# Seven products of quarters for eight in three of the six blocks of the last batch's wide product

## The chip, the cores and the metric

One core of one Trainium2 chip runs the whole kernel. The metric is the device time of one execution in microseconds (us), as the median over several runs. The profile is of one execution, with times in us from the start of its span. A core has five engines with a line of instructions each: TensorE (PE) multiplies, with its weight loads (PEld) beside it; VectorE (DVE), ScalarE (ACT) and GpSimd (POOL) work on elements; SyncE (SP) issues transfers, as ScalarE and GpSimd also do. Each engine takes its instructions in order. Between engines there are semaphores. Matmul results go to eight banks of 128 x 512 fp32; all else is in the large on-chip buffer, SBUF.

## The reference

A recurrent attention with decay (4 batches, 8 heads, 768 tokens, 64 channels a head) feeds a mixer over tokens and then one over channels:

```python
state = gamma[None, :, None, None] * state + np.einsum('bhd,bhe->bhde', k[:, :, t], v[:, :, t])
y[:, :, t] = scale * np.einsum('bhd,bhde->bhe', q[:, :, t], state)
...
xt = x.transpose(0, 2, 1)                       # x: 4 x 768 x 512
h = np.maximum(xt @ w_tok1, 0.0) @ w_tok2       # 768 -> 256 -> 768
u = x + h.transpose(0, 2, 1)
h2 = np.maximum(u @ w_ch1, 0.0) @ w_ch2         # 512 -> 1536 -> 512
return (u + h2).astype(np.float32)
```

The change is in `u @ w_ch1`, called the wide product here, for the last of the four batches. `h2`'s second half, from 1536 back to 512, is called the narrow product.

## The kernel before

**Planned order.** The kernel doesn't emit its work as it is written. It first makes a list of `Op`s, each with a priority, the engines it may run on with an estimated cost for each, the ops it depends on, the buffers it takes (`Slot`, with a tag) and uses. `arrange()` plans an order from the list greedily: at the earliest time at which something can start, it takes the op of best priority on that engine, picks an engine where there are several, a bank where one is needed, and a buffer of the tag when the oldest is given back. `guard` adds time to an op's earliest start, `behind` holds it back until another op is planned. `replay()` then runs through the order with a model of the transfers and gives a time. This is done 16 times with the transfers' times fed back, then once for each number in `SEEDS`, where `shake()` sets random delays on a few of the ops. The order with the best modelled time is emitted. So each engine's whole line, from the first instruction on, comes from this plan.

**Stages.** `front(b, p)` does the attention and the token mixer of batch b for the head pair p (four pairs of 128 channels). It leaves `X` (u in fp32, tokens on partitions) and `UT` (u in fp16, transposed: channels on partitions, four blocks `p` of 768 tokens). For batches 2 and 3 the transposing is done by a transfer that SyncE issues (line 752). L735 adds the token mixer's result to X; L656 and L743 are fp16 casts, mostly on GpSimd.

`back(b)` does the channel mixer. `widen(sh)` makes, for a half `sh` of the tokens (384 of 768), twelve blocks `ft` of 128 hidden channels: four matmuls of 128x384 over the four channel blocks into one bank (L818), then a relu on ScalarE to fp16 (L832) into `H2[:, ft]`. A batch has 24 such blocks, 96 matmuls. The tag `h2` has two buffers, one for each half of the tokens, and both are in use until the batch before has done its narrow product.

Batches 0 and 1 use `narrow(sh)` (L860, with its sum at L869). Batches 2 and 3 (`SEVEN = 2`) use `narrow_seven()`. There the matrices are cut into quarters (two halves of tokens, two halves of hidden channels, two halves of outputs), and Winograd's form of Strassen's method gives the four output quarters by seven products for eight, with some sums ahead and behind:

- `differences()`, L790: sums T1 to T4 of the quarters of `w_ch2`, on VectorE, 12 instructions, once, with the lowest priority
- `s_op`, L896: sums S1 to S4 of the quarters of H2, on VectorE, for two hidden blocks (and their two partners six blocks on) at a time: 12 instructions for each batch, in the tiles `kf`, `qf`, `v` and in H2 itself
- L937: seven products of six matmuls of 128x256 for each tile `i` of 128 tokens: p1 first (it needs only the lower halves), then others with the sums; S2 (tile `qf`), S1 (`kf`) and S4 (`v`) are their operands
- L964, L947, L990: a copy of p1's bank on ScalarE, and the sums of the products with X and with each other on VectorE, with GpSimd as an alternative for some; L955 stores

The banks have tags with ranges: `back` for banks 3 to 7, `seven` for all eight.

**Priority.** `front` ops have priority (0, ...), those of `back` (1, b, number in the batch), `differences` (2, ...).

Of the kernel before, what the change touches and what calls it, by code (L numbers as in the profile page):

```python
# [11 lines left out]
FP = mybir.dt.float32  # L12
F16 = mybir.dt.float16
AF = mybir.ActivationFunctionType
ALU = mybir.AluOpType
# [3 lines left out]
def kernel(  # L19
# [11 lines left out]
    nc = tc.nc  # L31
    B, H, S, D = q.shape
    P = 128
    NC = S // P
    HC = NC // 2
    NP = H // 2
    C = H * D
# [3 lines left out]
    NF = DC // P  # L41
    SH = S // 2
# [10 lines left out]
                uT=3, h2=2, o=4, w1=2)  # L53
    BANKS = dict(first=range(0, 7), front=range(0, 5), back=range(3, 8), seven=range(0, 8), fill=range(7, 8))
    SEM = 80
    XB, XU = 2, 2
    UNT, UW = 1, P
    QR, QH, TN = (0,), (1,), 3
    SEEDS = [20002, 20003, 20007, 20226]
    SPLIT, T1_AT, T2_AT = 1, 3, 4  # L60
    XS, M4 = 1, 3
    EARLY, BOTH_FIRST, SEVEN = 0, 1, 2
# [206 lines left out]
    def tile_of(slot, shape, dtype):  # L269
        if slot.bank is not None:  # L270
            slot.tile = ps.tile(shape, dtype, name=f"bank{slot.bank}", bufs=1)
        else:
            slot.tile = sb.tile(shape, dtype, name=slot.tag, bufs=BUFS[slot.tag])
        return slot.tile

    def act(n):
        t = 178 + 81 * n // 100
        return t - 100, t
# [7 lines left out]
    def one(eng, cost, emit):  # L286
        return [(eng, cost[0], cost[1], emit)]

    def either(emit, **costs):
        return [(e, c[0], c[1], lambda emit=emit, e=e: emit(e)) for e, c in costs.items()]  # L290
# [22 lines left out]
    def emit():  # L313
        nc.gpsimd.iota(away, pattern=[[1, P]], base=0, channel_multiplier=-1,
                       allow_small_or_imprecise_dtypes=True)
# [35 lines left out]
    NW = 3  # L351
    FW = NF // NW
    wc1 = [const_p.tile([P, NP, FW * P], F16, name=f"wc1_{i}") for i in range(NW)]
    wc2 = [const_p.tile([P, FW, C], F16, name=f"wc2_{i}") for i in range(NW)]
    wops = {}
# [15 lines left out]
    loads, x_done, uT_done, y_done, t2_done = {}, {}, {}, {}, {}  # L371
# [53 lines left out]
    def front(b, p):  # L425
# [154 lines left out]
        for blocks in runs:  # L580
            A = [Slot(FA) for _ in blocks]

# [215 lines left out]
    def back(b):  # L798
        X, UT = Xs[b], UTs[b]
        seq = [0]  # L800

        def op(ways, deps=(), takes=(), uses=(), dma=None):
            seq[0] += 1
            return Op((1, b, seq[0]), ways, deps, takes, uses, dma=dma)
        h2_of = {}

        def widen(sh):
            H2 = Slot("h2")
            rel = []
            fts = [f + g for f in range(0, NF // 2, 2) for g in (0, 1, NF // 2, NF // 2 + 1)]  # L810
            for ft in (fts if b >= SEVEN else range(NF)):
                A = Slot("back")

                def emit(cts, sh=sh, ft=ft, A=A):
                    acc = tile_of(A, [P, 512], FP) if cts[0] == 0 else A.tile
                    w = wc1[ft // FW]
                    for ct in cts:
                        nc.tensor.matmul(acc[:, :SH], w[:, ct, (ft % FW) * P:(ft % FW + 1) * P],  # L818
                                         UT.tile[:, ct, sh * SH:(sh + 1) * SH],
                                         start=(ct == 0), stop=(ct == NP - 1))  # L820
                cts = list(range(NP))
                c1 = None
                for part in (cts[:NP // 2], cts[NP // 2:]):
                    c1 = op(one("PE", (326, 480), lambda e=emit, q=part: e(q)),
                            [uT_done[b, p, sh] for p in (part if SPLIT > b else range(NP))] + [wops["c1", ft // FW], c1],
                            [A] if c1 is None else [], [UT] if c1 is None else [UT, A])

                def emit(e, ft=ft, A=A, H2=H2):
                    if H2.tile is None:
                        tile_of(H2, [P, NF, SH], F16)  # L830
                    if e == "ACT":
                        nc.scalar.activation(H2.tile[:, ft], A.tile[:, :SH], AF.Relu)  # L832
                    else:
                        nc.vector.tensor_scalar(H2.tile[:, ft], A.tile[:, :SH], 0.0, None, ALU.max)
                rel.append(op(either(emit, ACT=act(SH)),
                              [c1] + rel[:1], [H2] if ft == 0 else [], [A] if ft == 0 else [A, H2]))
            h2_of[sh] = H2, rel

        def narrow(sh):
            H2, rel = h2_of[sh]  # L840
# [168 lines left out]

        fts_of = [f + g for f in range(0, NF // 2, 2) for g in (0, 1, NF // 2, NF // 2 + 1)]  # L1010
        if b >= SEVEN:
            widen(0)
            widen(1)
            narrow_seven()
        elif b < BOTH_FIRST:
            widen(0)
            widen(1)
            narrow(0)
            narrow(1)
        else:  # L1020
            for sh in range(2):
                widen(sh)
                narrow(sh)
# [27 lines left out]
    for b in range(B):  # L1051
        back(b)
# [9 lines left out]
    best = None  # L1062
    for turn in range(16 + len(SEEDS)):
        if turn >= 16:
            shake(SEEDS[turn - 16])
        try:
            order = arrange()
            t = replay(order)
# [51 lines left out]
```

## Time and profile before

| What | Value |
|---|---|
| Median of 7 runs | 199.29 us (197.61 to 199.98) |
| The profiled execution | 199.98 us, of which the span is 198.2 us |
| Mean granted TensorE clock | 0.997 |
| Instructions | 4910 |
| Busy, TensorE / weight loads | 188.0 us (95%), 1951 matmuls / 130.9 us |
| Busy, VectorE | 131.2 us (66%) |
| Busy, ScalarE | 112.6 us (57%) |
| Busy, GpSimd | 82.7 us (42%) |
| Last transpose of the last batch's u (L752) | issued at 146.0 us, 2.7 us from issue to landing |
| Wide product of batch 3 (L818) | 12 matmuls from 154.2 us, 84 from 166.5 to 180.2 us |
| Narrow product of batch 3 (L937) | 180.2 to 194.1 us |

A matmul's busy time (326 ns for 128x384) is longer than the time from one to the next (84 of them take 13.65 us), since they overlap; a VectorE, ScalarE or GpSimd instruction also overlaps a little with the next. Therefore a price from a row is the time from start to end of one, and a price in a full line is the distance from one to the next. A wait is read from the idle time ahead of an instruction and its releaser.

### The profile page before, as it was taken

How to read it: one execution, taken by the hardware profiler on the slowest of the kernel's cores; microseconds unless marked ns; L12 is line 12 of the kernel's file. 1: busy time of each engine (PE TensorE's matmuls, PEld its weight loads, DVE VectorE, ACT ScalarE, POOL GpSimd, SP SyncE). 2: the span in 40 equal slices, each digit the busy share in tenths (PEclk: the TensorE clock that was granted, in tenths of full speed). 3: DMA queues.
4: the chain of work that ended last, by engine and by line, in shares of the span. 5: the costliest groups of instructions: out<-in, count | busy, mean ns of one | idle time of the engine just before them, and what ended most of it. 6: DMA issues, size and time to landing. Idle time of an engine off the chain costs nothing.

```text
span 198.2 us, 4910 instructions
## 1 busy us (share of the span) xinstructions
PE 188.0 (95%) x1951; PEld 130.9 (66%) x1951; DVE 131.2 (66%) x338; ACT 112.6 (57%) x251; POOL 82.7 (42%) x118
## 2 busy tenths in 40 slices
PE   7778899999999999899999999999999999999991
PEld 3456697566686675477575664576767787657881
DVE  6599681017899997757685925567289687048972
ACT  4368667899857664578642675248765002875000
POOL 7996876389789953427452210212320010000001
PEclk9999999999999999999999999999999999999998
DMA  7999999999999999999999991732030024100223
GB/s 120 144 169 177 209 205 207 177 155 149 149 149 179 170 160 198 130 201 168 135 157 88 221 158 36 171 71 40 20 65 3 0 106 159 56 0 0 106 110 106
DMA packets 97654, 24.89 MB, mean 126 GB/s; under 512 B 90208, under 2 KB 94688, under 8 KB 97632
## 3 DMA queue, kind: packets, MB, share of 16 engines
q0 software_dynamic: 73136, 13.18, 95.4%
q1 hardware_dynamic: 20896, 5.38, 21.3%
q10 hardware_dynamic: 3600, 6.03, 9.0%
q8 instruction: 15, 0.25, 0.6%
q14 instruction: 7, 0.06, 0.1%
HBM read 26.74 MB, written 6.29 MB: 167 GB/s over the span
## 4 chain that ended last, share of the span: by engine, by line
PE 57%; DMA 25%; POOL 8%; DVE 4%; issue 3%; ACT 0%; DVEq 0%; POOLq 0%
PE bank L818 24%; PE bank L937 14%; DMA kf<-in_k_dram 12%; DMA wc<-in_moe_w_ch_dram 9%; PE bank L860 9%; DMA wt<-in_moe_w_tok_dram 4%; POOL v L388 3%; PE bank L728 3%; PE bank L670 3%; PE bank L591 2%; PE bank L625 1%; POOL qf L406 1%; PE bank L621 1%; POOL kf L388 1%; POOL x L656 1%
## 5 line engine op out<-in xcount | busy, mean ns | idle before, releaser
L818 PE MATMUL bank<-uT,wc 128*128 128x384 f16 x384 | 69.3, 326 | 0.0
L832 ACT ACTIVATE h<-bank 128x384 f16<-128x384 f32 x96 | 45.3, 492 | 22.1 <-PE bank L818 16.0
L818 PEld LDWEIGHTS <-wc 128*128 128x128 f16 x384 | 35.6, 98 | 20.6
L860 PE MATMUL bank<-wc,h 128*128 128x512 f16 x144 | 36.7, 379 | 0.0
L605 DVE TENSOR_TENSOR am<-bank,mask 128x384 f16<-128x384 f32 x64 | 32.4, 549 | 4.8 <-PE bank L591 4.6
L656 POOL CAST x<-X 128x384 f16<-128x384 f32 x25 | 12.7, 511 | 30.3 <-ACT X L639 26.5
L639 ACT ACTIVATE X<-bank,gy 128x192 f32<-128x192 f32 x58 | 20.6, 419 | 6.0 <-PE bank L625 5.9
L735 DVE TENSOR_TENSOR X<-X,bank 128x384 f32<-128x384 f32 x30 | 15.8, 549 | 9.9 <-PE bank L728 9.7
L553 DVE SCALAR_TENSOR_TENSOR U<-U,gp,bank 128x128 f32<-128x128 f32 (+1 forms) x64 | 20.9, 326 | 1.5
L743 POOL CAST u<-X 128x384 f16<-128x384 f32 x27 | 13.4, 516 | 17.7 <-DVE X L735 17.5
L860 PEld LDWEIGHTS <-h 128*128 128x128 f16 x144 | 12.3, 98 | 9.5
L388 POOL DMA_DIRECT2D v<-in_v_dram x16 | 16.5, 1029 | 4.4 <-DMA kf<-in_k_dram 1.9
L564 ACT ACTIVATE r<-U 64x320 f16<-64x320 f32 x31 | 14.5, 467 | 5.9 <-DVE U L553 5.5
L388 POOL DMA_DIRECT2D kf<-in_k_dram x15 | 15.3, 1020 | 5.2 <-DMA qf<-in_q_dram 3.6
L937 PEld LDWEIGHTS <-h 128*128 128x128 f16 x144 | 14.1, 98 | 1.8
L670 PE MATMUL bank<-x,wt 128*128 128x128 f16 x192 | 13.6, 219 | 1.1 <-POOL x L656 0.8
L990 POOL TENSOR_TENSOR o<-o,w 128x256 f32<-128x256 f32 x1 | 1.0, 963 | 32.2 <-DVE w L947 32.2
L670 PEld LDWEIGHTS <-wt 128*128 128x128 f16 x192 | 11.9, 98 | 3.4 <-issue 1.6
L625 PEld LDWEIGHTS <-am 128*128 128x128 f16 x192 | 12.3, 98 | 2.9 <-DVE am L605 0.2
L625 PE MATMUL bank<-v,am 128*128 128x64 f16 x192 | 14.0, 193 | 0.0
L466 ACT ACTIVATE k<-kf,gk 128x384 f16<-128x384 f16 x16 | 9.8, 613 | 6.4 <-DMA kf<-in_k_dram 4.7
L728 PE MATMUL bank<-h,wt 128*128 128x128 f16 x180 | 13.3, 219 | 0.0
(93 smaller groups left out, 273.0 us busy)
## 6 DMA issues: line engine op xcount, KB each, us to landing
out_dram<-o ACTq DMA_DIRECT2D x22, 256.0 KB, 3.2
v<-in_v_dram POOLq DMA_DIRECT2D x16, 192.0 KB, 9.6
wc<-in_moe_w_ch_dram POOLq DMA_DIRECT2D x6, 512.0 KB, 15.4
kf<-in_k_dram POOLq DMA_DIRECT2D x15, 192.0 KB, 9.4
qf<-in_q_dram POOLq DMA_DIRECT2D x12, 192.0 KB, 8.9
wt<-in_moe_w_tok_dram POOLq DMA_DIRECT2D x2, 384.0 KB, 9.7
qf<-in_q_dram POOLq DMA_DIRECT2D x8, 96.0 KB, 8.7
X<-in_k_dram SPq DMA_DIRECT2D x1, 384.0 KB, 3.6
```

What stands on the lines that cost most here:

```text
L388: nc.gpsimd.dma_start(out=tile_of(s, [P, 2, NC, D], F16), in_=src[b, 2 * p:2 * p + 2].rearrange("h (c p) d -> p (h c) d", p=P))
L553: nc.vector.scalar_tensor_tensor(U[:, c, :W], U[:, c - 1, :W], gp[:, p:p + 1], o, ALU.mult, ALU.add)
L605: nc.vector.tensor_tensor(am[:, :m], src, k_, ALU.mult)
L625: nc.tensor.matmul(o[:, j * D:(j + 1) * D], M.tile[:, m], V.tile[:, j, c], start=(c == 0), stop=(c == 0 or j == 1))
L639: nc.scalar.mul(X.tile[:, half(hf), h * D:(h + 1) * D], yv[:, :, j * D:(j + 1) * D], gy[:, h:h + 1])
L670: nc.tensor.matmul(acc[:, jt * P:(jt + 1) * P], wt1[:, i, jt * P:(jt + 1) * P], X16.tile[:, i], start=(i == 0), stop=(i == NC - 1))
L728: nc.tensor.matmul(acc[:, i * P:(i + 1) * P], wt2[:, jt, t], H1.tile[:, jt], start=(jt == 0), stop=(jt == NJ - 1))
L735: nc.vector.tensor_tensor(xo, xo, T2.tile[:, :HC * P].rearrange("p (i d) -> p i d", d=P), ALU.add)
L818: nc.tensor.matmul(acc[:, :SH], w[:, ct, (ft % FW) * P:(ft % FW + 1) * P], UT.tile[:, ct, sh * SH:(sh + 1) * SH], start=(ct == 0), stop=(c ...
L832: nc.scalar.activation(H2.tile[:, ft], A.tile[:, :SH], AF.Relu)
L860: nc.tensor.matmul(A.tile, H2.tile[:, ft, i * P:(i + 1) * P], wc2[ft // FW][:, ft % FW], start=(opens and ft == 0), stop=(ft == NF - 1), s ...
L937: nc.tensor.matmul(bank.tile[:, cols], lhs(f, t), rhs(f), start=(f == 0 and not adds), stop=(f == HF - 1), skip_group_check=adds)
```

## The change

For batch 3 (`WIDE = 3`), `widen(0)` and `widen(1)` are replaced by `widen_seven()`. The six pairs of hidden blocks (q, q + 6) are each one small matrix product of quarters: two halves of tokens (`tok`), two halves of the channels that are summed over (`HP` = 2 blocks of 128 each), and the two hidden blocks q and q + 6. For q in `QUADS` = 1, 2, 4 the four output blocks (q and q + 6, both halves of tokens) come from seven products of two matmuls each; for q = 0, 3, 5 they are made as before, by `unit`, though in banks of the tag `seven`.

For the seven products there are sums ahead: T1 to T4 of the quarters of UT (four VectorE instructions of 128x768 fp16, in a buffer of tag `uT`), and S1 to S4 of the quarters of `w_ch1`'s blocks (three VectorE instructions of 128x256 fp16 each, in a buffer of tag `X`). T1 has a guard of 3000 ns in the plan. The sums of the weights have the priority (1, 2, 1) and are planned behind the first sum of batch 3's token mixer.

`quad` then has for each q the seven products in four banks, one copy on ScalarE, five VectorE sums in fp32 (two partial, three that are outputs), and four relus: one on ScalarE from a bank, three from SBUF on ScalarE or GpSimd (`relus`). `out` uses buffers of the tags k16, q16, kT and qT, which the attention no longer needs.

The relus of the other batches are as before; `unit` and `put` are `widen`'s body in functions of their own. `SEEDS` has four other numbers, so the plan of the whole kernel is drawn anew.

```diff
+    WIDE, QUADS, T_LATE = 3, [1, 2, 4], 3000
...
-    SEEDS = [20002, 20003, 20007, 20226]
+    SEEDS = [50147, 50148, 50150, 50217]
...
+            def bb(r, c):
+                return UT.tile[:, r * HP:(r + 1) * HP, tok[c]]
+
+            def aa(q, r, c):
+                ft = q + r * HF
+                return wc1[ft // FW][:, c * HP:(c + 1) * HP, (ft % FW) * P:(ft % FW + 1) * P]
+
+            def mix(k, todo, deps, m=1):
+                slot = T if k[0] == "T" else W
+                first = [made[x] for x in made if x[0] == k[0]][:1]
+
+                def emit():
+                    if slot.tile is None:
+                        tile_of(slot, [P, NP, S] if slot is T else [P, NC, 2 * C], F16)
+                    for o, x, y, alu in todo():
+                        nc.vector.tensor_tensor(o, x, y, alu)
+                made[k] = op(one("DVE", (200 * m, 200 * m + 90) if m > 1 else (480, 560), emit),
+                             deps + first, [] if first else [slot], ([slot] if first else []) + ([UT] if slot is T else []))
+                if k == "T1":
+                    made[k].guard = T_LATE
+                if slot is W:
+                    made[k].prio = (1, 2, 1)
+                    made[k].behind = x_done[B - 1, 0, 0]
...
+            mix("T1", lambda: [(tv("T1"), bb(0, 1), bb(0, 0), ALU.subtract)], ud)
+            mix("T2", lambda: [(tv("T2"), bb(1, 1), tv("T1"), ALU.subtract)], ud + [made["T1"]])
+            mix("T3", lambda: [(tv("T3"), bb(1, 1), bb(0, 1), ALU.subtract)], ud)
+            mix("T4", lambda: [(tv("T4"), bb(1, 0), tv("T2"), ALU.subtract)], ud + [made["T2"]])
...
+            mix("S1", each(lambda i, q: (wv("S1")[:, :, i], aa(q, 1, 0), aa(q, 1, 1), ALU.add)), cd, n)
+            mix("S2", each(lambda i, q: (wv("S2")[:, :, i], wv("S1")[:, :, i], aa(q, 0, 0), ALU.subtract)),
+                cd + [made["S1"]], n)
+            mix("S3", each(lambda i, q: (wv("S3")[:, :, i], aa(q, 0, 0), aa(q, 1, 0), ALU.subtract)), cd, n)
+            mix("S4", each(lambda i, q: (wv("S4")[:, :, i], aa(q, 0, 1), wv("S2")[:, :, i], ALU.subtract)),
+                cd + [made["S2"]], n)
+
+            def quad(i, q):
+                A, Bk, Ck, Dk = (Slot("seven") for _ in range(4))
+                W1, U2, U3 = Slot("u16"), Slot("x16"), Slot("x16")
...
+                p1 = mm(A, lambda c: aa(q, 0, 0)[:, c], lambda c: bb(0, 0)[:, c], True, ud + cd, [UT])
+
+                def emit():
+                    nc.scalar.copy(tile_of(W1, [P, SH], FP), A.tile[:, :SH])
+                w1 = op(one("ACT", act(SH), emit), [p1], [W1], [A])
+                p6 = mm(Bk, sv("S2"), lambda c: tv("T2")[:, c], True, [made["S2"], made["T2"]], [W, T])
+                u2 = add(U2, W1, Bk, [w1, p6], [])
+                p5 = mm(Ck, sv("S1"), lambda c: tv("T1")[:, c], True, [made["S1"], made["T1"]], [W, T])
+                p2 = mm(A, lambda c: aa(q, 0, 1)[:, c], lambda c: bb(1, 0)[:, c], False, [w1], [UT])
+                put(q, H2[0], rel[0], [p2], [A], lambda: A.tile[:, :SH], dict(ACT=act(SH)))
+                p4 = mm(Dk, lambda c: aa(q, 1, 1)[:, c], lambda c: tv("T4")[:, c], True, cd + [made["T4"]], [T])
+                p7 = mm(Bk, sv("S3"), lambda c: tv("T3")[:, c], False, [u2, made["S3"], made["T3"]], [W, T])
+                u3 = add(U3, W1, Bk, [p7], [])
+                relus = dict(ACT=act(SH), POOL=(500, 580))
+
+                def out(sh, ft, x, bank, deps):
+                    o = Slot(("k16", "q16", "kT", "qT")[temps[0] % 4])
+                    temps[0] += 1
+                    d = add(o, x, bank, deps, [])
+                    put(ft, H2[sh], rel[sh], [d], [o], lambda: o.tile, relus)
+                    return d
+                c22 = out(1, q + HF, U3, Ck, [u3, p5])
+                p3 = mm(Ck, sv("S4"), lambda c: bb(1, 1)[:, c], False, [c22, made["S4"]], [W, UT])
+                out(0, q + HF, U3, Dk, [u3, p4])
+                out(1, q, U2, Ck, [u2, p3])
+            for q in range(HF):
+                if q in QUADS:
+                    quad(QUADS.index(q), q)
+                else:
+                    for ft in (q, q + HF):
+                        for sh in range(2):
+                            unit(sh, ft, H2[sh], rel[sh], "seven")
...
         if b >= SEVEN:
-            widen(0)
-            widen(1)
+            if b >= WIDE:
+                widen_seven()
+            else:
+                widen(0)
+                widen(1)
             narrow_seven()
```

## The prediction

> **What bounds the kernel now.** I read the chain of waits first, from its end, because it says which engine the end hangs on. Its last pieces are (start, length, what):
>
> ```profile
> 144.46 6.50 PE bank L818 x40
> 150.96 3.27 PE bank L937 x30
> 154.24 1.95 PE bank L818 x12
> 156.19 10.48 PE bank L937 x96
> 166.67 13.65 PE bank L818 x84
> 180.32 13.78 PE bank L937 x132
> 194.12 0.29 DVE o L947
> 194.41 0.20 DVEq L1115
> ```
>
> From 144 us to 194 us one TensorE matmul follows another; no piece is a wait. L818 is the wide product, L937 the narrow one by sevens. The last batch's wide product is the 12 matmuls at 154.24, put in while the batch before waited for its sums, and the 84 at 166.67: 96 in all, and 13.65 / 84 = 0.1625 us each. So the change works on a stage where each matmul less moves the end by 0.1625 us, if no wait takes its place.
>
> Then the stretches, to see what the other engines have left (columns: busy time and count of each engine, clock, DMA share, GB/s):
>
> ```profile
> core 0: us, PE busy (x) PEld busy (x) DVE busy (x) ACT busy (x) POOL busy (x), PEclk, DMA share, GB/s
> 0.00:85.00 85.00, 78.88 (x929) 53.64 (x929) 59.34 (x176) 57.64 (x122) 62.41 (x83) 1.00 2.02 167
> 129.50:145.10 15.60, 15.60 (x186) 11.21 (x184) 8.48 (x19) 10.78 (x27) 4.19 (x9) 1.00 0.20 48
> 145.10:155.40 10.30, 10.30 (x76) 7.17 (x74) 10.24 (x25) 5.64 (x12) 0.90 (x2) 1.00 0.11 21
> 155.40:166.50 11.10, 11.10 (x101) 9.75 (x100) 8.62 (x19) 1.24 (x3) 0.73 (x1) 1.00 0.25 94
> 166.50:180.15 13.65, 13.65 (x86) 8.22 (x84) 4.59 (x11) 9.71 (x21) 0.00 (x0) 1.00 0.11 40
> 180.15:194.20 14.05, 13.94 (x134) 12.40 (x131) 11.61 (x26) 1.65 (x5) 0.90 (x1) 1.00 0.20 76
> ```
>
> TensorE is full in every row behind the first, at full clock. VectorE has no time left from 145.1 to 155.4 (0.06 us idle), and its large hole is in the stage that is changed: 13.65 - 4.59 = 9.06 us. GpSimd does nearly nothing behind 147 us.
>
> Last the groups and the forms, for the prices (minimum/median/maximum of one, in ns, for the lines with slashes):
>
> ```profile
> L832 ACT ACTIVATE h<-bank 128x384 f16<-128x384 f32 x96 | 45.3, 492 | 22.1 <-PE bank L818 16.0
> L735 DVE TENSOR_TENSOR X<-X,bank 128x384 f32<-128x384 f32 x30 | 15.8, 549 | 9.9 <-PE bank L728 9.7
> L656 POOL CAST x<-X 128x384 f16<-128x384 f32 x25 | 12.7, 511 | 30.3 <-ACT X L639 26.5
> L896 DVE TENSOR_TENSOR kf<-h x6: 543/550/557, 146.9 to 180.9; 128x768 f16<-128x768 f16 x6
> L790 DVE TENSOR_TENSOR wT<-wc x3: 410/464/718, 145.2 to 153.8; 128x512 f16<-128x512 f16 x3
> 181.47 0.56 DVE L896 TENSOR_TENSOR qf<-kf,h 128x768 f16<-128x768 f16 x1
> 182.77 0.82 PE L937 MATMUL bank<-wT,qf 128*128 128x256 f16 x6
> ```
>
> **The change, part by part.** *Matmuls.* Each of the three quads replaces four output blocks of four matmuls (16) by seven products of two (14), with the same 128x384 shape. 3 x 2 x 0.1625 = 0.975 us less on the path. The other 12 blocks keep their 48 matmuls; the stage goes from 96 to 90. This is the whole gain that the change can have in that stage, 0.49% of the median.
>
> *VectorE, sums of the quads.* Five for each quad (u2, u3 and three outputs), SBUF and bank in, 128x384 in fp32: the form of L735. One takes 0.549 us, and two in a row took 1.02 us, so a second costs 0.47. 15 sums are 7.05 us in a full row and 8.25 us if each must wait for the one ahead.
>
> *VectorE, sums of the tokens' halves (T1 to T4).* Four of 128x768 f16, the size of L896 at 0.55: 1.9 to 2.2 us.
>
> *VectorE, sums of the weights (S1 to S4).* Twelve of 128x256 f16, a size that the trace does not show. Above, L790 with 512 elements at 0.41 bounds it; below, the step from 512 to 768 elements (0.55 - 0.41 = 0.14 for 256) taken as if an instruction cost nothing but its elements. 12 x 0.14 = 1.7 us, 12 x 0.41 = 4.9 us; I take the straight line through the two rows, 0.27 each, 3.3 us. They depend on weights loaded long before, and on a buffer of tag X that batch 1 gives back when its last result sum ends, at 129.4. If they stand between 129.5 and 145.1 they lie in 15.60 - 8.48 = 7.1 us of hole and cost nothing. Queued behind them there are the front sums of the last batch; up to 3.3 us of delay to its tokens (the last transpose is issued at 146.0 and lands 2.7 us later) ends before their first use at 154.24. Without that hole they come behind 145.1 and are rival B.
>
> *ScalarE and GpSimd.* A copy of a 128x384 bank to fp32 for each quad is not shown; a 128x256 copy at 0.37 bounds it below, and I take L832's 0.49, which has its size, as the upper end. Of the 24 relus 15 stay with ScalarE and 9 may go to either. If all stay, 27 operations at 0.434 (seven in a row took 3.04) are 11.7 us in a stage of 12.7 to 14.6 us: hidden. On GpSimd a relu is costed at L656's 0.51, as cast of the same size; the one fp32 sum of 256 elements there took 0.73, which is the upper end. Both lie in an empty engine.
>
> The relus on GpSimd do meet VectorE: the first sum L790 at 145.2 ran beside a GpSimd cast and took 0.718 us against the usual 0.410, so a meeting costs 0.31 us. The quads' sums read one bank and one SBUF tile, as L735 does; at risk are the L896 sums, which read two SBUF tiles. Three meetings would be 0.9 us on VectorE's line; I take none into the sum, since ScalarE has room, and keep 0.9 for the upper end.
>
> The Trainium skill speaks against this part: "SBUF — State Buffer", section "Who interferes with whom", says that a VectorE instruction with two SBUF inputs and a GpSimd instruction that reads SBUF exclude each other for a whole instruction. By that rule each meeting costs up to a whole GpSimd relu, 0.51 us by the row above, where the one seen cost 0.31; the sum with three meetings would be 1.5 us in place of 0.9.
>
> *Chain inside a quad.* p1, copy, u2, p7, u3, c22, p3, an output sum, a relu: 0.49 + 0.49 + 0.55 + 0.49 + 0.55 + 0.55 + 0.49 + 0.55 + 0.49 = 4.65 us with rows' times (a pair of matmuls ends 0.326 + 0.1625 after its start), while its products fill TensorE for 14 x 0.1625 = 2.28 us. So two quads or a quad and plain blocks must run side by side. A quad takes four banks of eight, so that fits, and 12 plain blocks (7.8 us) are there to fill.
>
> *Hand-over to the narrow product.* Its third product needs the L896 sums of the last four blocks. Now qf is ready at 181.47 + 0.56 = 182.03 and used at 182.77: 0.74 us to spare. With VectorE behind by more than that, more of the first products of other tiles must be put in its place. For the waits that are left I choose 0.3 us: from 0 (the planner hides all) to 0.9 (the meetings above).
>
> *Queues and DMA.* No transfer is added or removed. H2's two buffers are held by batch 2's narrow product until 165.45, as now, so relus of blocks computed early wait, and their banks with them.
>
> **Sum.** -0.975 + 0.3 = -0.675. The profiled execution took 199.98 us (198.2 span, 1.78 around it): 199.3. It was 0.69 above the median 199.29, so in the median's terms **198.6 us**.
>
> **Rivals.** A is the forecast: 198.6, its own range 197.8 (waits 0, and 0.5 from a new order) to 199.5 (waits 0.9, and 0.3 from it). About 0.5%, 1.0 us, is what can be told from no change here; the seven runs reach from 197.61 to 199.98.
>
> B, *VectorE becomes the bound*. From 145.1 to the hand-over it has 0.06 + 2.48 + 9.06 = 11.6 us idle, less the 0.98 that is saved: 10.6. T and the quads' sums are 8.95 to 10.45. This just fits; with the weights' sums behind 145.1 it is 12.2 to 13.7, over by 1.6 to 3.1. With 2.3 late, of which TensorE covers perhaps 0.3 by other tiles' products, 199.29 - 0.98 + 2.0 = 200.3. It decides from the point at which L896 runs more than 0.74 us late. For it: VectorE in line at over 85% with dependent sums. Against: the hole before 145.1, and 14.05 - 11.61 = 2.4 us more behind 180.15 to catch up in.
>
> C, *T1 to T4 come too early*. VectorE's line is full to 155.4 with L790 and L896, and batch 2's third product waits for its end (the 12 matmuls at 154.24 fill that). T ahead of them, 2.2 us, puts that product off by as much; two free banks give cover for two blocks, 1.3 us at most, 0.65 if one is kept. 199.29 - 0.98 + 2.2 - 0.65 = 199.9. Against it: T1 is held back by 3 us in the plan.
>
> D, *the change is not what moves the time*. The seeds are new, so the whole order is. In the first 85 us TensorE is idle for 85 - 78.88 = 6.1 us. A fifth of it less is 1.2 us: 199.29 - 0.68 - 1.2 = 197.4. The same to the worse is as well possible, and lies in the upper part of B's range.
>
> **Chances.** A 0.46 (faster 0.27, same 0.17, slower 0.02); B 0.30 (slower 0.26, same 0.04); C 0.10 (slower 0.07, same 0.03); D 0.14 (faster 0.13, same 0.01). Faster 0.40, same 0.25, slower 0.35. The range, 197.3 to 201.0, leaves out the lower half of D and B with over 2.7 us lost, 0.13 together.
>
> **What would show it.** Right: six matmuls fewer from 144 us on; TensorE full from 85 us to its last product; the last wide block to the first narrow one without a hole; VectorE at 85 to 95% in the last wide stage; S1 to S4 before 145. Wrong: TensorE idle behind L937's first products with L896 as releaser (B); idle near 155 with L790 late (C); the first 85 us changed by more than the last 110 (D). A wait inside the quads, TensorE for VectorE's u2 or c22, would break the estimate of their chain.

## The result and the profile after

The changed kernel takes 200.69 us (median of 27 runs, 198.96 to 204.32) against 198.95 for the kernel before in 64 runs (197.57 to 201.31). The ratio is **1.0068, 95% interval 1.0041 to 1.0096**: slower by 0.8 to 1.9 us, about 1.35. (The ratio leaves out runs more than 1.5% above the fastest of their kernel, nine of 27 here and five of 64 before, so it isn't the quotient of the two medians, which is 1.0087, and it may put the loss too low.) The forecast was 198.6, faster by 0.3%; the time lies inside the range and on its wrong side.

Code behind the edit has moved: L818 is now L815, L937 is L1052, L896 is L1011, L605 is L606, L625 is L626, L477 is L478, L670 is L671, L947 is L1062. New are L875 (the sums T and S), L908 (the quads' products), L917 (their sums), L922 (their copy on ScalarE) and L834 (their relu on GpSimd; L832 remains ScalarE's).

First the stretches of the changed kernel, with the columns of those shown before:

```profile
core 0: us, PE busy (x) PEld busy (x) DVE busy (x) ACT busy (x) POOL busy (x), PEclk, DMA share, GB/s
0.00:85.00 85.00, 78.40 (x920) 52.48 (x921) 60.41 (x177) 56.23 (x120) 62.45 (x84) 1.00 2.01 166
129.50:142.80 13.30, 13.30 (x150) 9.37 (x149) 9.95 (x26) 8.27 (x21) 3.02 (x7) 1.00 0.21 51
142.80:153.70 10.90, 10.90 (x78) 7.54 (x77) 10.90 (x27) 7.11 (x15) 0.85 (x2) 1.00 0.10 20
153.70:164.20 10.50, 10.50 (x99) 9.40 (x97) 9.22 (x21) 0.37 (x1) 1.97 (x2) 1.00 0.26 100
164.20:179.10 14.90, 14.43 (x90) 8.59 (x88) 10.60 (x23) 9.61 (x21) 2.31 (x2) 1.00 0.10 36
179.10:193.40 14.30, 14.28 (x136) 12.59 (x133) 12.21 (x27) 2.38 (x7) 2.87 (x3) 1.00 0.20 75
```

TensorE is as full as before but for one row: in the changed stage, 164.2 to 179.1, 0.47 us of it is idle. Its busy time up to 85 us is 0.48 less than before, with the same clock.

The chain of waits (start, length, what) leaves TensorE at that place:

```profile
150.59 13.76 PE bank L1052 x126
164.35 2.60 PE bank L815 x16
166.95 2.29 PE bank L908 x14
...
172.31 1.18 POOL h L834
173.52 0.85 DVE kf L1011
174.37 0.48 DVE q L917
174.92 0.38 issue
175.30 0.47 ACT h L832
175.78 0.38 ACT u L922
176.19 0.48 PE bank L908 x2
177.33 1.95 PE bank L815 x12
...
180.26 13.13 PE bank L1052 x126
```

Where before one matmul followed another from 144 us on, the chain now goes through GpSimd's relu, VectorE, ScalarE's relu and copy. The releasers that TensorE waited for between 76 and 180 us (us in total, times, longest) are, after:

```profile
PE bank L626 <- DVE am L606: 1.2, 2, 1.0
PE bank L908 <- ACT u L922: 0.5, 1, 0.5
```

and before:

```profile
PE bank L670 <- POOL x L656: 0.8, 2, 0.6
```

**The spans can't be set against each other.** Two profiles of one and the same kernel further down (e7 and e12) have spans of 196.3 and 198.2 us, and the profiled execution of the changed kernel (199.83 us) lies below the median of its runs, while that of the kernel before (199.98) lies above. So three pieces of each profile are compared, each by itself: the waits up to the stage; the stage, from the first narrow matmul of batch 2 to the end of the last matmul; and the tail, from there to the end of the span.

| Piece | Before | After | Difference |
|---|---|---|---|
| TensorE's waits from 76 us to the stage | 0.8 | 1.2 | +0.4 |
| Stage | 150.96 to 194.08: 43.12 | 150.59 to 193.37: 42.78 | -0.34 |
| Tail | 4.12 | 4.73 | +0.61 |

The stage is 0.34 shorter where six matmuls less are 0.975: 0.64 us came back in it. The tail, which the prediction held to be fixed, is longer (a tail is good to 0.05, since the span is given to a tenth).

The stage is the firm piece. In the profiles of all kernels of this document, those further down too, it is 43.12 or 43.13 us with the old products (six profiles), 42.77 to 42.79 with the quads and three of their relus on GpSimd (four), and 42.14 or 42.15 with all relus on ScalarE (four). What lies ahead of it varies between executions of one kernel, and by more than the waits of the first row: in this pair of profiles the changed kernel's stage starts 0.37 us earlier than that of the kernel before, in a second pair 2.67 us later (e3 and e4, 153.06 and 150.39).

**The wait at 82 us.** The timeline (start, length, engine, line, operation, count; in brackets the idle time ahead of it and what ended it) of the changed kernel:

```profile
81.10 0.36 DVE L478 COPY q<-qf 128x768 f16<-128x768 f16 x1 [1.89 <-DMA qf<-in_q_dram]
81.38 1.95 DVE L606 TENSOR_TENSOR am<-bank,mask 128x384 f16<-128x384 f32 x4
...
81.99 0.20 PE L626 MATMUL bank<-v,am 128*128 128x64 f16 x1 [0.96 <-DVE am L606]
```

and of the kernel before:

```profile
81.50 0.83 ACT L475 COPY q<-qf 128x768 f16<-128x768 f16 x1 [1.52 <-DMA qf<-in_q_dram]
...
83.65 0.33 PE L670 MATMUL bank<-x,wt 128*128 128x128 f16 x3 [0.57 <-POOL x L656]
```

It is one instruction, the cast of batch 2's last q (head pair 3), whose load lands late in both. In the new order it stands on VectorE ahead of four masks for batch 2's first head pair. The masks' inputs are there, but VectorE takes its line in order, stands 1.89 us, and TensorE waits for the masks. Before, the cast stood on ScalarE, ahead of scalings of X; the masks ran at 78.08, and the wait fell on the token mixer (L670) by way of GpSimd's cast. Both orders pay for the late load, at different places.

**The tail.** The last matmul of the changed kernel is at

```profile
192.54 0.83 PE L1052 MATMUL bank<-wc,v 128*128 128x128 f16 x12
```

and the transfers of its last 3.6 us (queue, kind: packets, MB, share of 16 engines) are

```profile
q1 hardware_dynamic: 144, 0.26, 20.5%
q10 hardware_dynamic: 333, 0.16, 14.6%
q14 instruction: 1, 0.01, 0.5%
```

The first two are stores. The third is a piece of program being loaded, which starts at 195.3 us in the trace. In the kernel before the last piece on that queue started at 188.5, and there are seven in all where there now are eight. The last stores take longer from issue to landing. This is the store that SyncE issues (KB, us), before and after:

```profile
out_dram<-o SPq DMA_DIRECT2D x1, 256.0 KB, 2.3
out_dram<-o SPq DMA_DIRECT2D x1, 256.0 KB, 2.9
```

### The profile page after: what moved, and what is told of

It is laid out like the page before. It is cut to its first block, busy times and chain, and to the rows that moved or that the text cites. A ratio compares the mean times of both kernels' runs of the same rounds, so it can differ in the third digit from the quotient of the medians.

```text
span 198.1 us, 4930 instructions
## 1 busy us (share of the span) xinstructions
PE 186.3 (94%) x1941; PEld 129.1 (65%) x1941; DVE 145.3 (73%) x372; ACT 110.8 (56%) x247; POOL 89.0 (45%) x123
## 4 chain that ended last, share of the span: by engine, by line
PE 56%; DMA 27%; POOL 8%; DVE 4%; issue 3%; ACT 0%; DVEq 0%; POOLq 0%
PE bank L815 19%; PE bank L1052 14%; DMA qf<-in_q_dram 13%; PE bank L975 9%; DMA wc<-in_moe_w_ch_dram 9%; DMA wt<-in_moe_w_tok_dram 4%; PE bank L671 3%; PE bank L729 3%; POOL v L389 2%; PE bank L908 2%; PE bank L626 2%; POOL kf L389 2%; PE bank L592 2%; PE bank L622 1%; POOL qf L407 1%
## 5 line engine op out<-in xcount | busy, mean ns | idle before, releaser
L815 PE MATMUL bank<-uT,wc 128*128 128x384 f16 x336 | 61.0, 326 | 0.0
L832 ACT ACTIVATE h<-bank 128x384 f16<-128x384 f32 x87 | 40.9, 490 | 18.5 <-PE bank L815 15.6
L815 PEld LDWEIGHTS <-wc 128*128 128x128 f16 x336 | 31.1, 98 | 18.0
L606 DVE TENSOR_TENSOR am<-bank,mask 128x384 f16<-128x384 f32 x64 | 32.5, 548 | 4.8 <-PE bank L592 4.8
L640 ACT ACTIVATE X<-bank,gy 128x192 f32<-128x192 f32 x60 | 21.8, 418 | 11.4 <-PE bank L626 11.2
L744 POOL CAST u<-X 128x384 f16<-128x384 f32 x29 | 14.7, 521 | 20.3 <-DVE X L736 17.4
L657 POOL CAST x<-X 128x384 f16<-128x384 f32 x23 | 11.9, 516 | 25.1 <-ACT X L640 14.2
L626 PE MATMUL bank<-v,am 128*128 128x64 f16 x192 | 15.0, 193 | 2.1 <-DVE am L606 2.0
L565 ACT ACTIVATE r<-U 64x320 f16<-64x320 f32 x29 | 13.6, 467 | 5.6 <-DVE U L554 5.1
L626 PEld LDWEIGHTS <-am 128*128 128x128 f16 x192 | 12.6, 98 | 5.9 <-DVE am L606 3.3
L1052 PEld LDWEIGHTS <-h 128*128 128x128 f16 x144 | 14.1, 98 | 1.9
L671 PE MATMUL bank<-x,wt 128*128 128x128 f16 x192 | 13.4, 219 | 0.6 <-DMA wt<-in_moe_w_tok_dram 0.6
L469 DVE TENSOR_SCALAR k<-kf,gk 128x384 f16<-128x384 f16 x15 | 5.3, 365 | 11.5 <-DMA kf<-in_k_dram 11.5
L729 PEld LDWEIGHTS <-wt 128*128 128x128 f16 x180 | 11.4, 98 | 3.1
L671 PEld LDWEIGHTS <-wt 128*128 128x128 f16 x192 | 11.6, 98 | 2.1 <-DMA wt<-in_moe_w_tok_dram 0.8
## 6 DMA issues: line engine op xcount, KB each, us to landing
v<-in_v_dram POOLq DMA_DIRECT2D x16, 192.0 KB, 9.2
kf<-in_k_dram POOLq DMA_DIRECT2D x15, 192.0 KB, 9.5
qf<-in_q_dram POOLq DMA_DIRECT2D x12, 192.0 KB, 8.9
```

The lines of the kernel that those rows point to most:

```text
L606: nc.vector.tensor_tensor(am[:, :m], src, k_, ALU.mult)
L626: nc.tensor.matmul(o[:, j * D:(j + 1) * D], M.tile[:, m], V.tile[:, j, c], start=(c == 0), stop=(c == 0 or j == 1))
L640: nc.scalar.mul(X.tile[:, half(hf), h * D:(h + 1) * D], yv[:, :, j * D:(j + 1) * D], gy[:, h:h + 1])
L671: nc.tensor.matmul(acc[:, jt * P:(jt + 1) * P], wt1[:, i, jt * P:(jt + 1) * P], X16.tile[:, i], start=(i == 0), stop=(i == NC - 1))
L729: nc.tensor.matmul(acc[:, i * P:(i + 1) * P], wt2[:, jt, t], H1.tile[:, jt], start=(jt == 0), stop=(jt == NJ - 1))
L832: nc.scalar.activation(H2.tile[:, ft], src(), AF.Relu)
```

## The experiments

The planner draws a new order whenever the list of work changes, so an edit would move everything. Except for e3 and e4, each kernel therefore emits an order that is written down as a literal list (number of the op, engine, banks) in place of the planner's:

```diff
-    for o, o.start, o.end, o.eng, o.emit, at in best[1]:
+    for item in PLAN.split():
+        head, start = item.split(":")
+        o = ops[int(head[:n])]
+        o.eng = dict(P="PE", D="DVE", A="ACT", G="POOL", S="SP")[head[n]]
...
+        order.append(o)
```

**e1 and e2: the order apart from the products.** e1 is the changed kernel in which the order ahead of the planned time 124 us is that of the kernel before; e2 is the kernel before with the changed kernel's order ahead of 124 us.

> The changed kernel with the order of every instruction planned to start ahead of 124 us taken from the kernel before, and the rest, the seven products among it, in the changed kernel's own order. Theory 1 (the new seeds' order of the first 124 us loses what is lost, the seven products gain about 0.4 us): 197.9 to 198.6 us, a ratio of 0.995 to 0.999 to the kernel before. Theory 2 (the seven products' stage loses it): 199.7 to 200.3, a ratio of 1.005 to 1.009.

Measured: 201.86 us (6 runs), ratio 1.0176 (1.0116 to 1.0236); neither theory's range holds.

> The kernel before, without the seven products of the wide stage, but with the changed kernel's order of what is planned to start ahead of 124 us. Theory 1 (order): it loses as the changed kernel does or a little more, 199.9 to 200.6 us, ratio 1.006 to 1.011. Theory 2 (products): 198.3 to 198.9, ratio 0.998 to 1.002.

Measured: 201.71 us (6 runs), ratio 1.0128 (1.0081 to 1.0175), above theory 1's range with its interval reaching into it. In its profile TensorE waits 2.4 us for the masks at 82 us, with the old work behind.

Neither total tells the order from the products, since both joints cost something themselves: in e1 TensorE is idle 2.3 us between 120 and 140 us (1.0 for GpSimd's casts, 0.6 for sums), in e2 0.8 us for a sum at the joint. e1 decides nothing. e2 shows that the wait for the masks comes with the new order alone, without a single quad: 2.4 for the masks, 0.8 for the joint, 0.65 for a tail of 4.77 and some 0.9 saved at L670 give 2.95 us, where 0.0128 x 199.54 = 2.55 was measured; the profiled execution, at 202.47 us, was one of the longer ones.

**e3 and e4: both kernels once more,** unchanged.

> The changed kernel as it is, for a second profile beside the others. Both theories: near 200.0 us. Theory 1 expects its last matmul to end later than in the kernel before of the same call because the stages ahead of 124 us end later; theory 2 expects the delay behind 164 us.

Measured: 202.48 us (10 runs), ratio 1.0139 (1.0094 to 1.0185). The expected 200.0 was missed, and the same kernel had a ratio of 1.0068 above: ratios from different sets of runs, on different chips, are not to be compared more finely than that.

> The kernel before as it is, for a second profile: its first one, at 199.98 us, lay 1.5 us above the median of its runs. Both theories: 197.6 to 198.5 us in most runs. Theory 1 expects the difference between its two profiles to lie ahead of 85 us, where its chain of waits hangs on the loads; theory 2 does not say.

Measured: 199.43 us, one run, with a tail of 4.19 and 1.0 us of wait at L670. As theory 1 has it, e3 is late ahead of the stage (2.67 us against e4 at its start) and not in it. In e3 the stage is 42.78 and the tail 4.67, as in the first profile, but the load is later still. Its timeline:

```profile
82.20 0.36 DVE L478 COPY q<-qf 128x768 f16<-128x768 f16 x1 [3.20 <-DMA qf<-in_q_dram]
...
83.08 0.24 PE L626 MATMUL bank<-v,am 128*128 128x64 f16 x1 [2.29 <-DVE am L606]
```

The same wait is 2.29 us here and 0.96 there; with the second mask's it is 2.5 against 1.2. What follows it is seen in e3's stretches:

```profile
82.00:83.00 1.00, 0.00 (x0) 0.00 (x0) 0.80 (x3) 0.00 (x0) 0.53 (x1) 1.00 1.91 162
83.00:84.00 1.00, 0.69 (x8) 0.57 (x9) 1.00 (x4) 0.00 (x0) 0.49 (x1) 0.52 1.37 301
...
85.00:86.00 1.00, 1.00 (x12) 0.83 (x11) 0.01 (x1) 0.48 (x1) 0.51 (x1) 0.50 1.59 126
86.00:87.00 1.00, 1.00 (x12) 0.80 (x10) 0.38 (x2) 0.74 (x3) 0.04 (x1) 0.78 2.45 156
```

TensorE stands for the whole of 82 to 83, and the granted clock (third number from the end) is then 0.5 for 3.4 us. e3 is 2.47 us later than the first profile at its first narrow matmul of batch 2 (153.06 against 150.59); 2.29 - 0.96 = 1.33 of this is the longer wait, and the rest was not taken apart further, though a stretch at half clock lies in it.

**e5: the cast behind the masks,** in the changed kernel. Entry 453 is the cast, 366 to 369 are the four masks, D is VectorE:

```diff
 63G:79765
-453D:79077
 350P0:80088
 366D:79871
...
 369D:81275
+453D:79077
```

> The changed kernel in its own order, with one cast moved: batch 2's last q to fp16 (L478) goes on VectorE from ahead of four mask products (L606) to behind them. Theory 1 (the cast waits for a load that lands late, and the masks and TensorE's L626 stand behind it): TensorE's wait for L606 near 82 us, 1.2 and 2.5 us in the two profiles of the changed kernel, is gone or under 0.3 us; 1 to 2 us faster than the changed kernel, a ratio of 0.995 to 1.002 to the kernel before. Theory 2 (the stage of the seven products loses the time): no change, ratio 1.007 to 1.014.

Measured: 199.35 us (12 runs), ratio 1.0026 (0.9987 to 1.0065). Its timeline:

```profile
79.93 1.95 DVE L606 TENSOR_TENSOR am<-bank,mask 128x384 f16<-128x384 f32 x4 [0.26 <-PE bank L592]
...
81.80 0.35 DVE L478 COPY q<-qf 128x768 f16<-128x768 f16 x1
```

The masks run as soon as their bank is there, the load has landed when its cast is reached, and TensorE waits for no mask. What is left of its waits is the 0.5 us at L908; the stage is 42.77 and the tail 4.66, as in the changed kernel. But the load was early in this execution: GpSimd, which waits for the same load, goes on at 80.65, and at 81.38 and 82.47 in the two profiles of the changed kernel. So this trace alone doesn't show that the place does it. Those of e9 and e10 further down do, which have the cast in the same late place: there the load was as late as in e3, the cast starts at 82.50 and 82.33 (82.20 in e3) after a wait of 0.80 and 0.59, and TensorE waits for no mask. The size is not told by the times: 1.0068 and 1.0026 have intervals that overlap, and come from different sets of runs.

**e6, e7 and e12: the same cast in the kernel before.** e6 puts it on VectorE ahead of the masks, as the changed kernel has it; e7 on VectorE behind them; e12 is e7 once more.

```diff
 350P0:76392
 397A:76626
+453D
 366D:76607
...
 63G:77880
-453A:77880
 369D:78011
```

> The kernel before in its own order, with the same cast moved the other way: from ScalarE to VectorE, ahead of the four mask products. Theory 1: it takes over the changed kernel's loss, 1 to 2 us, ratio 1.005 to 1.010, with TensorE waiting for the masks near 81 us. Theory 2: ratio 0.998 to 1.002.

Measured: 199.15 us (12 runs, 197.81 to 203.96), ratio 0.9982 (0.9938 to 1.0026): not slower. Its timeline:

```profile
78.83 0.36 DVE L477 COPY q<-qf 128x768 f16<-128x768 f16 x1 [1.77 <-DMA qf<-in_q_dram]
...
79.71 0.20 PE L625 MATMUL bank<-v,am 128*128 128x64 f16 x1 [0.69 <-DVE am L605]
```

The wait for the masks is there (0.69 + 0.26), but the load was early in this execution, and the wait at L670 (0.8 to 1.0) is gone since ScalarE no longer holds the cast. One wait took the place of the other, and my expectation, which counted only the new one, missed. What the same order costs when the load is late was not seen: four of the 12 runs took 201.88 to 203.96 us and are not in the ratio, and none of them was profiled.

> The kernel before with the same cast taken from ScalarE to VectorE, behind the four mask products: the same place as in the first run of this call, so that the two differ by the seven products and the rest of the order. Theory 1: ratio 0.997 to 1.002, and 0 to 0.5 us slower than the first run if the products give what TensorE's stage shows (0.35 us). Theory 2: 1 us or more faster than the first run.

Measured: 198.38 us (12 runs), ratio 1.0005 (0.9959 to 1.0051). In its profile (span 196.3) TensorE waits nowhere over 0.2 us from 76 to 180. It was expected no faster than e5 and is 0.97 us faster by the medians, 0.2% by the ratios: by the traces e5's stage is 0.36 shorter than e7's and its tail 0.58 longer.

> The kernel before with the cast late and no seven products in the wide stage, on the same chip as the run ahead. If moving the cast alone is a gain: ratio 0.992 to 0.998; if the cast costs the kernel before nothing: 0.998 to 1.002.

Measured: 199.86 us (12 runs), ratio 1.0008 (0.9958 to 1.0058). Its timeline shows why the clean profile of e7 brought nothing in the times:

```profile
81.35 0.36 DVE L477 COPY q<-qf 128x768 f16<-128x768 f16 x1 [1.38 <-DMA qf<-in_q_dram]
...
84.24 0.66 PE L670 MATMUL bank<-x,wt 128*128 128x128 f16 x9 [0.72 <-POOL x L656]
```

When the load is late, whoever stands next in the line waits, wherever the cast is put. The place decides only whether that is something TensorE needs at once. Between the kernel before and its two variants no place is better by what these times can tell; the changed kernel's place, with masks that TensorE needs behind it, costs 1.2 and 2.5 us in its two profiles (cast at 81.10 and 82.20), where the kernel before paid 0.8 and 1.0 (cast at 81.50 and 80.92).

**e8: the relus of the quads all on ScalarE,** on top of e5. Three entries change their engine, G (GpSimd) to A:

```diff
-1045G:171168
+1045A:171168
...
-1057G:171668
+1057A:171668
...
-1089G
+1089A
```

> As the first run, and the three relus that the plan gave to GpSimd (L834, 1.15 to 1.34 us each) run on ScalarE in the same place of the order. Theory 3 (they are slow, hold the sums L1011 and, through the output sum behind those and the relu behind that, the third quad's copy L922, for which TensorE waits 0.47 us): that wait is gone and the wide stage is 0.4 to 0.6 us shorter than in the first run, ratio 0.992 to 0.999. Against it: the wait stays within 0.1 us.

Measured: 198.65 us (12 runs), ratio 1.0005 (0.9970 to 1.0040), where at most 0.999 was expected. In the changed kernel's timeline the stage had gone thus:

```profile
172.31 1.17 POOL L834 TENSOR_SCALAR h<-kT 128x384 f16<-128x384 f32 x1 [15.21 <-DVE kT L917]
...
173.47 1.15 POOL L834 TENSOR_SCALAR h<-qT 128x384 f16<-128x384 f32 x1
...
173.52 0.85 DVE L1011 TENSOR_TENSOR kf<-h 128x768 f16<-128x768 f16 x1 [0.45 <-POOL h L834]
...
174.30 0.54 DVE L917 TENSOR_TENSOR q<-x,bank 128x384 f32<-128x384 f32 x1
...
174.87 0.52 ACT L832 ACTIVATE h<-q 128x384 f16<-128x384 f32 x1 [0.87 <-DVE q L917]
...
175.67 0.47 ACT L922 COPY u<-bank 128x384 f32<-128x384 f32 x1
...
176.19 0.48 PE L908 MATMUL bank<-uT,wc 128*128 128x384 f16 x2 [0.47 <-ACT u L922]
```

Five engines' lines are to be read in turn. GpSimd's first relu takes 1.17 us; the sum kf waits 0.45 for it, then runs beside the second relu and takes 0.85 where it takes 0.55 alone; the quad's output sum behind it on VectorE is late, ScalarE's relu waits 0.87 for that sum, the third quad's copy stands behind this relu, and TensorE waits 0.47 for the bank that the copy gives back. In e8 the same two steps are

```profile
174.20 0.49 ACT L922 COPY u<-bank 128x384 f32<-128x384 f32 x1
...
174.74 0.49 PE L908 MATMUL bank<-uT,wc 128*128 128x384 f16 x2
```

with no bracket, so no wait, and the stage is 149.78 to 191.92 = 42.14 us: 0.98 less than the 43.12 of the kernel before, the six matmuls to a hundredth. Against e5 (42.77) the three relus were worth 0.63 in the stage. All of it is lost at this one place, and the idle time of 0.47 is only part of it: from the start of the pair of matmuls ahead of the wait to the start of the pair behind it the changed kernel takes 0.95 us (175.24 to 176.19), e8 0.32 (174.42 to 174.74). The times moved by 0.2%, with overlapping intervals, since the tail of e8 is 4.98 where e5 has 4.66. Nor is the order ahead free of late loads: TensorE waits 0.3 us in e8, 0.7 in e9 and 0.9 in e11 near 90 us at L622, for ScalarE's X (L640), which stands in ScalarE's line behind a scaling of k (L467) that waited 0.7, 1.1 and 1.3 us for its load.

**e9 and e10: the end of the program.** To e8, eight copies of one element are added whose result nobody uses, on ScalarE near 151 us (e9) or on VectorE near 165 us (e10). They do no work but make that engine's program longer.

```diff
+    scratch = const_p.tile([P, 1], F16, name="scratch")
...
+        if o is ops[1006]:
+            for _ in range(8):
+                nc.vector.tensor_copy(scratch, zero[:, :1])
```

(e9 has `nc.scalar.copy` and another op.)

> As the last run (cast late, all relus on ScalarE), with eight copies of one element more on ScalarE near 151 us, where it waits some 5 us anyway. Theory 4 (ScalarE's line has become seven instructions shorter, so that the load of the last piece of its program comes behind the last matmul and the end waits for it): that load, one packet of the queue q14 some 2 us behind the last matmul, moves ahead of it; from the last matmul to the end of the span 4.1 to 4.2 us in place of 4.98; 0.6 to 0.8 us faster, ratio 0.993 to 0.998. Against it: the packet stays behind the last matmul and the tail at 4.6 to 5.0.

Measured: 198.72 us (12 runs), ratio 1.0024 (0.9991 to 1.0058); tail 5.00. Theory 4 is refuted.

> The same eight copies of one element on VectorE near 165 us, where it is idle for 3 us, and none on ScalarE. Theory 4, the load is ScalarE's: the tail stays at 4.6 to 5.0 us, ratio 0.997 to 1.003. Theory 4b, it is VectorE's: the tail is 4.1 to 4.2 us here and stays long with the copies on ScalarE. If the tail has nothing to do with that load both stay.

Measured: 198.05 us (12 runs), ratio 0.9976 (0.9938 to 1.0013); tail 4.09, as theory 4b has it. The transfers of e10's last 3.6 us:

```profile
q10 hardware_dynamic: 432, 0.26, 23.5%
q1 hardware_dynamic: 144, 0.26, 19.6%
```

No piece of program is among them any more. Where the late pieces on that queue start in each kernel, and the tail:

| Kernel | Late program pieces start at (us) | Last matmul ends | Tail |
|---|---|---|---|
| before | 188.5 | 194.08 | 4.12 |
| after | 192.0 and 195.3 | 193.37 | 4.73 |
| e8 | 189.5 and 194.3 | 191.92 | 4.98 |
| e9, copies on ScalarE | 175.7 and 195.1 | 192.70 | 5.00 |
| e10, copies on VectorE | 189.3 and 190.2 | 191.71 | 4.09 |

Copies on ScalarE move the earlier of e8's two pieces, copies on VectorE the last. So the last is VectorE's program, and wherever it lies behind the last matmul (e1, e2, e3 and e5 too: 4.66 to 4.95) the tail is 0.5 to 0.9 us longer than where it lies ahead (e4, e6, e7 too: 4.08 to 4.19). It isn't the quads' sums as such that bring it there: e2 has the old products, 342 VectorE instructions where the changed kernel has 372 and the one before 338, and its tail is long (4.77). Where the last boundary falls differs from kernel to kernel here.

The traces also show what is late in the long tails: the last stores. SyncE's store of 256 KB lands 2.2 to 2.3 us after its issue and ScalarE's two of 64 KB 2.1 to 2.2 in all seven profiles with a short tail. In the seven with a long one, SyncE's takes 2.9 to 3.0 and ScalarE's 2.5 to 2.6 (after, e2, e3, e5), or ScalarE's 2.7 to 2.8 at SyncE's 2.3 (e1, e8, e9).

**e11: the same kernel as e10 again,** beside e12.

> The version that all findings point to (seven products, cast late, relus on ScalarE, eight small copies on VectorE), beside the next run on one chip, to tell what the seven products are worth when nothing else eats them. If the six matmuls saved reach the end: 0.5 to 1.0 us faster than the next run and a ratio of 0.993 to 0.999 to the kernel before. If the rest of its order costs as much: no difference to the next run.

Measured: 198.52 us (12 runs), ratio 0.9967 (0.9931 to 1.0003); tail 4.07. Against e12 the mean over the runs that the ratios count is 0.84 us lower (198.34 and 199.18), as expected. The ratios of e10 and e11, weighted by their intervals, give 0.9971 (0.9945 to 0.9997). So with the cast behind the masks, the relus on ScalarE and the copies, the change comes out 0.3% faster than the kernel before, about 0.6 us. That is the edge of what these times can tell: the interval only just leaves out no change, the version is one picked from several, and e10's median is 198.05 where the kernel before, run beside it, has 197.84. Against the changed kernel as it was (1.0068) it is 1% faster, with intervals well apart.

## Why the prediction was wrong

**What became of the sum,** from stage pieces and not from spans (the third row counts TensorE's waits alone, from two pairs of profiles):

| Term | Predicted | Shown |
|---|---|---|
| Six matmuls | -0.975 | -0.98 (e8 against before) |
| Waits in the stage | +0.3 | +0.64 (42.78 - 43.12 + 0.98) |
| New order ahead of the stage | 0 | +0.4 to +1.5 (waits 1.2 - 0.8; in e3 and e4 2.5 - 1.0) |
| End of the span | 0 | +0.55 (4.70 - 4.15, means of two each) |
| Sum | -0.675 | +0.6 to +1.7; the times say +1.35 (0.8 to 1.9) |

**The step that failed first** is "The same to the worse is as well possible, and lies in the upper part of B's range". I had read that the whole order is drawn anew, and 6.1 us of idle TensorE in the first 85 us; then I gave the good half of that a case of its own, in which slower had no chance at all, and put the bad half into a case of another mechanism. In the sum it stands at nothing, and 0.3 us is all that the forecast's own range allows for it. The bad half came: 0.4 and 1.5 us in waits. It could be read ahead of time in kind, though not in place: the profile of before shows a q load that lands at 81.5 and holds ScalarE for 1.52 us, so an order that puts that cast ahead of something that TensorE needs at once can be made to wait by it. The new order is no part of the products, but it is a part of the change.

**The second** is a size: "On GpSimd a relu is costed at L656's 0.51, as cast of the same size". The forms of the changed kernel (minimum/median/maximum in ns):

```profile
L834 POOL TENSOR_SCALAR h<-qT x2: 1153/1244/1336, 173.5 to 179.8; 128x384 f16<-128x384 f32 x2
```

The shape was right and the operation was not: a maximum against zero takes GpSimd 2.3 times as long as a cast. The upper end, 0.73 from "the one fp32 sum of 256 elements there", was too low as well: scaled by elements it is 1.1 for 384, an estimate, and there were two such sums in that profile; the other (L990) took 0.963, which scales to 1.4. "I take none into the sum, since ScalarE has room" then fell: the planner, whose estimate for it is 500 to 580 ns, did use GpSimd. The mechanism, a relu on GpSimd that disturbs an L896 sum, was named, with a price of 0.31 for each meeting; it was seen once, at 0.85 - 0.55 = 0.30. Two of the weights' sums that ran beside GpSimd casts, at 132.6 and 133.7 us, took 0.591 and 0.584 where the others took 0.28, 0.31 more as well. That agrees with the row and not with the rule of the Trainium skill ("SBUF — State Buffer", "Who interferes with whom"), by which the sum would have been held for the whole rest of the relu: the relu started first, at 173.47 against 173.52, and ran to 174.62, and the sum ended inside it, at 174.37. What TensorE felt was mainly the relu's own length in a chain without slack.

**The third** was not thought of: "199.98 us (198.2 span, 1.78 around it)" was carried over as it stood. I looked at the work up to the last store and never at what else lies behind the last matmul. The Trainium skill, "Runtime: NRT & Kernel Launch", section "Instruction fetch mechanics", says that an engine's program is streamed in blocks by its own queue and that the cost of crossing a block is mostly hidden. No wait in the profile of before is put down to the seven pieces of this queue, which agrees; the one behind the last matmul goes with 0.5 to 0.9 us, which doesn't.

**What held.** The whole gain of the products is in e8's stage to a hundredth. VectorE is no bound (rival B): it is at 71% in the stage, less than the 85 to 95% that I gave as a sign of being right, and the last sum qf is ready at 182.60 and first used at 183.37, 0.77 to spare where I had read 0.74 before. T1 to T4 are no bound either (rival C): they run at 151.0 to 156.5 among the L1011 sums, and TensorE is full from 142.8 to 164.2. The prices of the sums and their hole:

```profile
L875 DVE TENSOR_TENSOR X<-wc x3: 284/285/292, 132.0 to 132.4; 128x256 f16<-128x256 f16 x3
L875 DVE TENSOR_TENSOR uT<-uT x4: 545/548/754, 151.0 to 155.8; 128x768 f16<-128x768 f16 x4
```

The straight line through two rows gave 0.27 for the first (two of the twelve took twice that, as said), and 0.55 was read for the second; the weights' sums are all done by 135.1, in the hole ahead of 145. Rival D named one of the three terms that were missing, and had its sign wrong.

**What stays open.** Why the last stores land later when a piece of VectorE's program is loaded beside them; that they do, and that moving the piece ahead takes it back, is shown. How the +1.35 divides between the order and the end by times alone, since each single step from the changed kernel to e5, e8 and e10 (0.4, 0.2, 0.3%) is no larger than its interval; only the whole way from 1.0068 to 0.9971 is. Whether the order alone makes the time longer when the products are left as they were: e2 says yes, but has a joint and a long tail of its own, and e6 says no, with an early load. And why the load of that q lands where it does: e7 and e12 are one kernel, in one TensorE waits nowhere and in the other the load is late, and they are 1.9 us apart.

## What to carry to other kernels

If a change makes a planner draw a new order, cost the order as an item of its own with both signs: look for instructions that wait for late loads, and for who stands behind them on the same engine. Take a price from a row of the same operation, not only of the same shape, above all on GpSimd. Compare by stages with marks in the trace (first and last matmul of a stage, end of the span), since here the spans of one kernel differ by twice what the change is worth.

## What the hardware showed that I had not expected

- A maximum against zero, 128x384 fp32 to fp16, took GpSimd 1.15 to 1.34 us; a cast of that shape 0.51 there, the relu 0.49 on ScalarE.
- A TensorE idle of 2.29 us was followed by a granted clock of 0.5 for 3.4 us (e3); one of 2.10 us (e2) and one of 0.96 (after) were not, so what decides is not told here. The Trainium skill, "TensorE: Matmul & The Clock Gate", Part 1, has the clock fall after one idle window of about 3.4 us; here less was enough in one execution.
- A piece of VectorE's program that is loaded behind the last matmul goes with a tail of 4.66 to 5.00 us, and 4.07 to 4.19 where it is loaded ahead; in the first case some of the last stores take 0.5 to 0.8 us longer to land. Eight copies of one element on that engine were enough to move it.
